# Reordering the opening of a fused attention and two-layer MoE kernel: q, k and v before most weights

## The chip, the core and the metric

The kernel runs on one core of a Trainium2 chip. The time is the device time of one execution in microseconds, and the median of three runs is what counts. Engines: PE is the matrix engine, DVE the vector engine, ACT the scalar engine, POOL the GpSimd engine; SP issues most of the transfers, ACT's queue the rest.

## What is computed

Three stages follow one another on 4608 tokens of width 512:

```python
# attention inside chunks of 64 tokens, 8 batches x 8 heads x 576 tokens x 64
scores = matmul(q_c, k_c^T) / sqrt(64);  scores -= max(scores)
attn = exp(scores);  attn /= sum(attn) + 1e-9
x = matmul(attn, v_c)                      # 4608 x 512 after the heads are put side by side
# gated layer, 512 -> 1536 -> 512
xn = x / sqrt(mean(x*x) + 1e-6) * rms_g
y = (silu(xn @ w_gate) * (xn @ w_val)) @ w_out
# second layer, 512 -> 2048 -> 512
h = y @ w_in;  out = (h * clip(h + 3, 0, 6) / 6) @ w_out2
```

The weights come as 64-bit floats. A load brings the raw words, and the kernel turns them into a float32 and splits that in a high and a low part.

## The kernel before

Tokens are worked in nine blocks of 512. Block 0 is the stretch that matters here. Its attention is done first, in four tiles of 128 tokens (class `Att`, `first[0]` to `first[3]`). Then its gated layer runs in a loop over twelve slices f of the hidden width (lines 1208 to 1223), while the attention of later blocks and the conversion of the remaining weights go on beside it. All engines work their instructions in the order of the program, which is written out by hand (`manual_schedule`).

**The opening** follows two lists. `LOADS` is the order of the first transfers on SP's queue: `w` is the next of 36 weight pieces of 512 KB (gate, val and out of slice 0, of slice 1, and so on: piece 3f is gate f, 3f+1 is val f, 3f+2 is out f), `q0` loads q and k of tile 0 (256 KB each), `v0` its v in four transfers. `START` is the order of the steps. A step ending in a digit belongs to that tile: `trans_qk` turns q and k on PE, `out_q` and `out_k` copy them back on ACT, `scores` (PE), `top` and `less` (DVE: maximum, subtraction), `expo` (ACT), `total` (DVE), `share` (POOL), `trans_p` (PE), `out_p` (ACT), `values` (PE), `out_x` and `square` (ACT), `squares` (POOL), `mean` (PE), `root` (ACT), `inv` (DVE), `spread` (PE), `norm` (DVE), `hi` (ACT, writes XH) and `lo` (POOL, writes XL). XH and XL of all four tiles are what block 0's matmuls read.

**Weight conversion** has four stages for a piece: `m` (ACT, `mag`, L164), `b` (DVE, `bits`, four instructions, L171 to L179), `h` (ACT, `hi`, L186) and `l` (DVE, `lo`, L195). A token `Wb1` does the stage for piece 1; `wb1` does it for pieces 2 and 3, which is group 1; group g is pieces 2g and 2g+1, and there are 18 groups. What `START` leaves is done inside block 0 by `prep_a.step()`. The loop has 36 thirds, hk 0 to 35; third 0 of a slice is the gate product, third 1 the val product and then `sg` (silu times val, DVE, L1215) and its split (`ah` on ACT, L975; `al` on POOL, L976), third 2 the down product of the slice before. After each third `tick()` puts out the planned steps of attention and normalisation, and after every even third `step()` puts out, in this order, lo of one group, hi of the next, bits of the next and mag of the next. At the first step the kernel before has groups 0 to 6 begun and groups 0 to 4 finished, so step s (at hk 2s) does lo of group 4+s and bits of group 6+s.

**What else sits in that loop.** The attention of tokens 512 and on goes in pairs of tiles (class `Pair`): pair 2 starts at hk 7, pair 3 at hk 19, pair 4 at hk 31, with `turn_q` and `turn_k` (DVE, L683) first, `scores`, `top`, `less`, `expo` three thirds later, `total` and `share` two later, `trans_p` and `out_p` at +8, `values`, `out_x` and `square` at +9, `squares` at +11. Between the two lists and the loop, the kernel queues on SP 16 further weight pieces, and after each of the first twelve of them four of the 48 small transfers of pair 2's q and k. The normalisation of block 1 (`Rms(1)`) is planned for hk 31 and 32: `halve`, `mean`, two reciprocals and four products on DVE. `sg` has one buffer, so silu of slice f+1 (ACT) waits until `al` of slice f has read it.

```python
for third in range(3):
    if third == 1:
        mm_up(VB, whole(W["val", f]), xs)
        nc.vector.tensor_tensor(s, s, PS[:, VB, :], op=ALU.mult)
        a = split_act(s)
    elif third == 2 and prev is not None:
        mm_down_a(W["out", f - 1], prev, f == 1, False)
    tick()
    if b == 0:
        prep_hook(hk)
```

Of the kernel before, what the change touches and what calls it, by code (L numbers as in the profile page):

```python
# [18 lines left out]
def _f32_of(word):  # L19
# [7 lines left out]


LOADS = """
    w q0 q1 w w w q2 w q3 v0 w v1 w w w v2 w w w v3 w w w w  # L30
""".split()
START = """
    Wm0 Wb0 Wh0 Wl0 Wm1 trans_qk1 trans_qk0 out_q0 out_k0 wm1 Wb1 scores0 top0 Wh1 out_k1 less0 wb1 out_q1 Wl1 expo0
    trans_qk2
    out_q2 total0 scores1 top1 share0 less1 out_k2 scores2 top2 trans_p0 wh1 wl1 trans_qk3 expo1 wm2 less2
    out_p0 values0 total1 expo2 share1 out_q3 trans_p1 total2 out_k3 out_p1 scores3 square0 share2 wb2 top3
    values1 trans_p2 wm3 out_x0 less3 out_x1 square1 squares0 mean0 out_p2 squares1 values2 expo3 mean1 root0
    total3 out_x2 share3 wb3 inv0 wm4 trans_p3 square2 root1 inv1 wh2 out_p3 wb4 values3 out_x3 squares2
    square3 mean2 spread1 norm1 spread0 root2 squares3 mean3 wl2 inv2 root3 wh3 hi1 spread2 norm0 inv3 wm5
    norm2 hi2 lo1 spread3 hi0 lo2 norm3 hi3 lo3 wh4 wm6 lo0 wl3 wb5 wb6 wh5 wl4  # L40
""".split()

STEPS_P = (
# [1619 lines left out]
```

## Time and profile before

| what | value |
|---|---|
| median of three runs | 1726.3 us (1726.11 to 1726.57) |
| the profiled execution | 1722.63 us, of which the span of instructions is 1720.8 us |
| PE busy | 1656.4 us, 96% of the span |
| DVE busy | 1092.9 us, 64% |
| ACT busy | 843.4 us, 49% |
| POOL busy | 493.5 us, 29% |
| mean granted clock of PE | 0.989 of full speed |

The busy shares are means over the whole span. In the page's 40 slices of 43 us each, PE reads 4, 7, 8 and then 9 in every slice but the last, and DVE reads 7, 9, 9, 7 in the first four: the opening looks unlike the rest and has to be read by itself.

### The profile page before, as it was taken

To read this page: it belongs to the slowest core of one execution; us is meant where nothing else is said; L and a number is where in the kernel's file an instruction comes from. 1 tells how busy PE (TensorE), PEld (TensorE's weight loads), DVE (VectorE), ACT (ScalarE), POOL (GpSimd) and SP (SyncE) were. 2 spreads that over 40 slices of the span, in tenths; PEclk is the share of its full clock that TensorE was granted. 3 is DMA by queue.
4 is the path that set the end of the run, shared out by engine and by line. 5 is a ranking of instruction groups with operands and counts; after the bars stand their busy time and mean duration, and the time that the engine had idled before them with its cause. 6 is when DMAs were issued, how large, how long until landed. Compare 5 with 4: busy or idle time off the path is not lost.

```text
span 1720.8 us, 26448 instructions
## 1 busy us (share of the span) xinstructions
PE 1656.4 (96%) x9896; PEld 1355.6 (79%) x9896; DVE 1092.9 (64%) x1548; ACT 843.4 (49%) x1359; POOL 493.5 (29%) x360
## 2 busy tenths in 40 slices
PE   4789999999999999999999999999999999999998
PEld 4568777787887888887887878888888888888887
DVE  7997655757657586666544468548735754773474
ACT  5554434544554544553534324456545554664553
POOL 2322333430224532265224632231014002301310
PEclk8799999999999999999999999999999999999999
DMA  9832676645798768974778867667766676676664
GB/s 251 231 83 53 198 223 181 175 151 181 235 303 256 216 222 282 296 263 161 276 282 297 291 239 242 220 196 228 237 198 219 220 228 187 222 234 204 196 198 145
DMA packets 291839, 375.06 MB, mean 218 GB/s; under 512 B 132864, under 2 KB 215808, under 8 KB 291584
## 3 DMA queue, kind: packets, MB, share of 16 engines
q1 hardware_dynamic: 230272, 303.11, 57.0%
q10 hardware_dynamic: 61440, 70.27, 12.1%
q8 instruction: 78, 1.28, 0.3%
q14 instruction: 49, 0.40, 0.1%
HBM read 292.55 MB, written 80.74 MB: 217 GB/s over the span
## 4 chain that ended last, share of the span: by engine, by line
PE 51%; DVE 1%; DMA 0%; issue 0%; ACT 0%; ACTq 0%; POOL 0%; SPq 0%; DVEq 0%; POOLq 0%
PE PS L932 24%; PE PS L1461 18%; PE PS L921 2%; PE PS L949 1%; PE PS L946 1%; PE PS L947 1%; PE PS L1478 1%; PE PS L954 1%; PE PS L955 1%; PE PS L958 1%; DMA x<-yd 0%; DVE xf L882 0%; DVE xt L1134 0%; DVE sraw L252 0%; DVE sc L243 0%
## 5 line engine op out<-in xcount | busy, mean ns | idle before, releaser
L932 PE MATMUL PS<-xu,wo 128*128 128x512 f32 x1512 | 351.9, 392 | 2.8 <-DVE gu L1239 2.3
L932 PEld LDWEIGHTS PS<-xu,wo 128*128 128x128 f32 x1512 | 281.5, 188 | 64.3 <-DVE gu L1239 3.1
L1461 PE MATMUL PS<-gs,wq 128*128 128x512 f32 x1344 | 308.5, 390 | 0.0
L932 PE MATMUL PS<-xo,wq 128*128 128x512 f32 x1344 | 306.1, 389 | 0.0
L932 PEld LDWEIGHTS PS<-xo,wq 128*128 128x128 f32 x1344 | 252.0, 188 | 52.2
L1461 PEld LDWEIGHTS PS<-gs,wq 128*128 128x128 f32 x1344 | 251.4, 188 | 51.6
L921 PE MATMUL PS<-XH,w 128*128 128x512 f32 x576 | 149.1, 400 | 11.3 <-DVE sg L1215 5.4
L976 POOL TENSOR_TENSOR al<-sg,ah 128x512 fp32r<-128x512 f32 x52 | 80.5, 1548 | 230.4 <-ACT ah L975 226.1
L921 PEld LDWEIGHTS PS<-XH,w 128*128 128x128 f32 x576 | 108.5, 191 | 39.6 <-DVE sg L1215 6.8
L946 PE MATMUL PS<-gs,wd 128*128 128x512 f32 x288 | 113.6, 394 | 2.1 <-DVE gu L1239 1.6
L947 PE MATMUL PS<-gs,wd 128*128 128x512 f32 x288 | 112.2, 389 | 0.0
L1513 POOL TENSOR_TENSOR gt<-gx 128x512 f32<-128x512 f32 x8 | 10.3, 1291 | 306.3 <-DVE gx L1510 306.3
L1235 POOL TENSOR_TENSOR gs<-gu,gs 128x512 fp32r<-128x512 f32 x60 | 84.8, 1432 | 45.9 <-ACT gs L1234 39.6
L1455 DVE TENSOR_TENSOR gs<-gu,gs 128x512 fp32r<-128x512 f32 x88 | 68.2, 794 | 42.0 <-ACT gs L1454 41.2
L1239 DVE TENSOR_TENSOR gu<-gu,PS 128x512 f32<-128x512 f32 x60 | 40.9, 685 | 76.0 <-ACT gu L1321 40.6
L975 ACT CAST ah<-sg 128x512 fp32r<-128x512 f32 x52 | 32.3, 621 | 99.5 <-DVE sg L1215 67.2
L1392 DVE SCALAR_TENSOR_TENSOR gu<-gu,PS 128x512 f32<-128x512 f32 x48 | 32.8, 684 | 72.9 <-ACT gu L1389 72.9
L921 PE MATMUL PS<-XL,w 128*128 128x512 f32 x288 | 78.9, 396 | 0.0
L949 PE MATMUL PS<-gs,wd 128*128 128x512 f32 x288 | 77.1, 390 | 0.8 <-POOL gs L1235 0.8
L1454 ACT CAST gs<-gt 128x512 fp32r<-128x512 f32 x96 | 58.2, 624 | 38.0 <-DVE gt L1582 28.2
L1454 ACT CAST gs<-gu 128x512 fp32r<-128x512 f32 x96 | 57.7, 622 | 24.8 <-DVE gs L1455 17.8
L1513 POOL TENSOR_TENSOR gt<-gu 128x512 f32<-128x512 f32 x24 | 32.5, 1356 | 129.0 <-DVE gu L1510 124.8
(228 smaller groups left out, 2884.9 us busy)
## 6 DMA issues: line engine op xcount, KB each, us to landing
wq<-stash_in SPq DMA_DIRECT2D x128, 512.0 KB
wo<-ops SPq DMA_DIRECT2D x126, 512.0 KB
wq<-sums_out SPq DMA_DIRECT2D x64, 512.0 KB
wq<-stash_out SPq DMA_DIRECT2D x48, 512.0 KB
wd<-keep_out SPq DMA_DIRECT2D x36, 512.0 KB
ops<-w ACTq DMA_DIRECT2D x36, 256.0 KB
yd<-yst SPq DMA_DIRECT2D x18, 512.0 KB
sraw<-in_moe_w_in_dram ACTq DMA_DIRECT2D x16, 512.0 KB
```

Of the source, the lines that this page charges most:

```text
L921: nc.tensor.matmul(ps, w(wi, c), xs[c][xi], start=(i == 0), stop=(i == n - 1))
L932: nc.tensor.matmul(PS[:, bank, :], op[:, wi, c * 128:(c + 1) * 128], x[xi][:, c, :], start=first and i == 0, stop=last and i == 5, skip_gr ...
L946: nc.tensor.matmul(ps, wm[0], a[0], start=first, stop=False)
L947: nc.tensor.matmul(ps, wm[1], a[0], start=False, stop=False)
L949: nc.tensor.matmul(PS[:, banks[m], :], w[:, 0, m * 128:(m + 1) * 128], a[1], start=False, stop=last)
L976: nc.gpsimd.tensor_tensor(lo, t, hi.bitcast(F32), op=ALU.subtract)
L1235: nc.gpsimd.tensor_tensor(w[:, 1, :], t, w[:, 0, :].bitcast(F32), op=ALU.subtract)
L1239: nc.vector.tensor_tensor(o, x, y, op=op)
L1454: nc.scalar.copy(w[:, 0, :], x)
L1455: e.tensor_tensor(w[:, 1, :], x, w[:, 0, :].bitcast(F32), op=ALU.subtract)
L1461: nc.tensor.matmul(PS[:, banks[m], :], op[:, wi, m * 128:(m + 1) * 128], x[xi], start=first and (wi, xi) == (0, 0), stop=False, skip_group ...
L1513: nc.gpsimd.tensor_tensor(slot(i, "t"), slot(i, "12"), slot(i, "11"), op=ALU.subtract)
```

## The change

Only the two lists change; no instruction is added or dropped. In `LOADS` the q and k of all four tiles and all of v come after at most three weight pieces, and the other thirteen pieces follow. In `START` the steps of attention stand as early as their inputs allow and nearly all conversion tokens stand behind them. Pieces 0 and 1 are converted as before; of the pairs, mag goes to group 3 instead of 6, bits to 2 instead of 6, hi to 1 instead of 5, and lo of groups 1 to 4 is no longer there. So step s of the loop now does lo of group 1+s, hi of 2+s, bits of 3+s and mag of 4+s, three groups (six pieces) behind the kernel before, and ends with lo of group 17 at hk 32 instead of hk 26.

```diff
 LOADS = """
-    w q0 q1 w w w q2 w q3 v0 w v1 w w w v2 w w w v3 w w w w
+    w q0 q1 q2 w q3 v0 w v2 v1 v3 w w w w w w w w w w w w w
 """.split()
 START = """
-    Wm0 Wb0 Wh0 Wl0 Wm1 trans_qk1 trans_qk0 out_q0 out_k0 wm1 Wb1 scores0 top0 Wh1 out_k1 less0 wb1 out_q1 Wl1 expo0
-    trans_qk2
-    out_q2 total0 scores1 top1 share0 less1 out_k2 scores2 top2 trans_p0 wh1 wl1 trans_qk3 expo1 wm2 less2
-    out_p0 values0 total1 expo2 share1 out_q3 trans_p1 total2 out_k3 out_p1 scores3 square0 share2 wb2 top3
-    values1 trans_p2 wm3 out_x0 less3 out_x1 square1 squares0 mean0 out_p2 squares1 values2 expo3 mean1 root0
-    total3 out_x2 share3 wb3 inv0 wm4 trans_p3 square2 root1 inv1 wh2 out_p3 wb4 values3 out_x3 squares2
-    square3 mean2 spread1 norm1 spread0 root2 squares3 mean3 wl2 inv2 root3 wh3 hi1 spread2 norm0 inv3 wm5
-    norm2 hi2 lo1 spread3 hi0 lo2 norm3 hi3 lo3 wh4 wm6 lo0 wl3 wb5 wb6 wh5 wl4
+    Wm0 trans_qk0 out_q0 out_k0 scores0 Wb0 trans_qk1 out_q1 out_k1 top0 less0 Wh0 scores1 expo0 trans_qk2
+    out_q2 out_k2 top1 less1 expo1 total0 share0 scores2 trans_p0 top2 less2 expo2 out_p0 trans_qk3 total1
+    total2 share1 values0 out_q3 Wl0 out_k3 scores3 out_x0 top3 square0 less3 trans_p1 out_p1 Wm1 squares0 expo3
+    values1 share2 square1 out_x1 trans_p2 out_p2 squares1 mean0 total3 share3 Wb1 values2 root0 out_x2 square2
+    trans_p3 out_p3 squares2 mean1 root1 inv0 values3 square3 spread0 inv1 out_x3 norm0 squares3 mean2 root2
+    spread1 inv2 norm1 hi0 lo0 mean3 root3 spread2 inv3 norm2 hi1 lo1 spread3 hi2 Wh1 norm3 Wl1 lo2 hi3 lo3 wm1
+    wb1 wm2 wh1 wm3 wb2
 """.split()
```

## Rows read from the trace of the kernel before

**Rows 1.** Busy time by stretch (length, then each engine; granted clock, transfer share, GB/s).
```profile
0.00:56.30 56.30, 25.34 (x320) 20.89 (x320) 43.33 (x91) 29.85 (x55) 13.66 (x24) 0.78 0.96 249
61.90:120.00 58.10, 46.74 (x257) 36.11 (x255) 54.43 (x98) 30.89 (x49) 17.08 (x6) 0.97 0.57 146
120.00:183.50 63.50, 62.88 (x506) 51.17 (x506) 50.61 (x72) 31.87 (x45) 11.78 (x8) 0.97 0.26 56
```

**Rows 2.** Busy time, 24.2 to 56.3: all instructions; on wtmp (DVE, ACT); on w.
```profile
24.20:56.30 32.10, 15.97 (x199) 13.15 (x196) 29.90 (x66) 19.70 (x39) 11.47 (x13) 0.61 0.97 266
24.20:56.30 32.10, 15.49 (x24) 5.07 (x8) 0.61 0.97 266
24.20:56.30 32.10, 0.00 (x0) 0.00 (x0) 3.40 (x5) 2.57 (x5) 0.00 (x0) 0.61 0.97 266
```

**Rows 3.** PE in order of time: start, length, line, operation [idle before, releaser].
```profile
24.26 1.85 PE L507 MATMUL PS<-ident,q 128*128 128x128 f32 x8
56.31 3.78 PE L921 MATMUL PS<-XH,w 128*128 128x512 f32 x8 [1.92 <-ACT XH L623]
119.95 1.99 PE L763 MATMUL PS<-qT,v 64*64 64x64 f32 x64 [3.00 <-ACT qT L751]
157.62 1.16 PE L763 MATMUL PS<-qT,v 64*64 64x64 f32 x64
166.11 1.07 PE L921 MATMUL PS<-XL,w 128*128 128x512 f32 x4
173.70 1.98 PE L921 MATMUL PS<-XH,w 128*128 128x512 f32 x8
```

**Rows 4.** DVE in order of time, the same columns.
```profile
68.52 0.68 DVE L1215 TENSOR_TENSOR sg<-sg,PS 128x512 f32<-128x512 f32 x1
89.33 1.20 DVE L683 STREAM_TRANSPOSE kT<-k 128x1024 f32<-128x1024 f32 x1
111.61 0.67 DVE L1215 TENSOR_TENSOR sg<-sg,PS 128x512 f32<-128x512 f32 x1
119.03 0.69 DVE L1215 TENSOR_TENSOR sg<-sg,PS 128x512 f32<-128x512 f32 x1 [1.78 <-ACT sg L1211]
143.40 1.28 DVE L195 TENSOR_TENSOR w<-wraw,w 128x512 fp32r<-128x512 f32 x2
144.60 0.76 DVE L171 TENSOR_SCALAR wtmp<-wtmp 128x512 f32<-128x512 f32 x2
148.35 1.21 DVE L731 TENSOR_REDUCE sm<-p 128x16 f32<-128x1024 f32 x1
152.83 0.67 DVE L1215 TENSOR_TENSOR sg<-sg,PS 128x512 f32<-128x512 f32 x1
157.80 0.69 DVE L1215 TENSOR_TENSOR sg<-sg,PS 128x512 f32<-128x512 f32 x1 [3.09 <-PE PS L921]
167.28 0.69 DVE L1215 TENSOR_TENSOR sg<-sg,PS 128x512 f32<-128x512 f32 x1 [4.29 <-PE PS L921]
176.11 2.74 DVE L882 SCALAR_TENSOR_TENSOR xf<-xf,g_sb,rt 128x512 f32<-128x512 f32 x4
```

**Rows 5.** POOL in order of time: `al` of slices 4 and 5.
```profile
113.02 5.34 POOL L976 TENSOR_TENSOR al<-sg,ah 128x512 fp32r<-128x512 f32 x1 [5.63 <-ACT ah L975]
120.49 1.56 POOL L976 TENSOR_TENSOR al<-sg,ah 128x512 fp32r<-128x512 f32 x1 [2.13 <-ACT ah L975]
```

**Rows 6.** ACT in order of time: the copy behind silu of slice 5.
```profile
118.89 1.01 ACT L751 COPY qT<-PS 128x1024 f32<-128x1024 f32 x1
```

**Rows 7.** Transfers in order of time: issues on SP, and a PE load that waited.
```profile
5.57 1.05 SPq L491 DMA_DIRECT2D q<-in_k_dram  x1
10.44 2.42 PEld L507 LDWEIGHTS PS<-ident,q 128*128 128x128 f32 x12 [0.24 <-DMA q<-in_k_dram]
50.22 0.39 SPq L157 DMA_DIRECT2D wraw<-in_moe_w_gate_dram  x1
76.81 2.80 SPq L668 DMA_DIRECT2D k<-in_k_dram  x4
```

## Prediction

> **What bounds the kernel now.** I read the busy time by stretch first, because the 96% of PE is a mean over stages [rows 1]. From 120 to 183.5 us PE works 62.88 of 63.50 us; before 120 it is idle for 31.0 of the first 56.3 us and 11.4 of the 58.1 from 61.9 to 120. So nearly all that can be won in block 0 lies before 120 us. DVE is the other engine to look at: it works 43.33 of the first 56.3 us and 54.43 of the 58.1 after 61.9. The second view is each engine in order of time. PE starts block 0's first product at 56.31, when XH is there [rows 3]. The product of slice 0 on DVE (`sg`) comes at 68.52, and later ones at 111.61, 119.03 and 152.83 with DVE busy without a gap in most of the stretches between [rows 4]. PE's last long wait in block 0 ends at 119.95 [rows 3]. So from 24 us to about 153 us DVE sets the pace, and only from `sg` of slice 9 (157.80, where DVE waits 3.09 us for PE) is PE ahead in the argument, with DVE idle in places. Where the work is paced by DVE, a conversion that is moved is not saved: it must fit into a later hole of DVE, and be done before PE asks for its piece.
>
> I use "old time" below for a moment of the trace of before; the new moment is the old one, less the shift of the head, plus what the tail adds.
>
> **Part 1, the head: the start of block 0.** Between 24.2 and 56.3 DVE is busy 29.90 us, of which 15.49 are `bits` and 3.40 are `lo` that lie wholly inside, 18.9 together [rows 2]. The new list keeps `bits` of one piece and `lo` of two in that place, about 15.49/6 + 2*0.68 = 3.9 us. So DVE work falls by 15.0 us; and tile 3's turn, at 24.26 now [rows 3], can stand some 4 us earlier, since only the loads and three tiles' first steps precede it. Floor for the first product: 56.31 - 15.0 - 4 = 37. But then DVE no longer bounds the opening, and a chain through PE, ACT, POOL and DVE does, with a wait at each step; nothing in the trace shows that chain bare. The upper end is that only half of the 19 us is won: 46.8. I take 43, two thirds of the gain, 13.3 us. The loads allow it: the last of q and k of tile 1 was issued by 6.62 and PE had it at 10.44 [rows 7], and the pace of 249 GB/s [rows 1] brings the 4.7 MB up to v of tile 3 by some 22 us.
>
> Behind the last `norm`, DVE now has `bits` of groups 1, 2 and 3 and `lo` of group 1 ahead of `sg` 0. One burst of `bits` is 148.35 - 144.60 = 3.75 us and one `lo` pair 144.60 - 143.40 = 1.2 us [rows 4], so 3*3.75 + 1.2 = 12.45, with XH's start about 1 us before. Now it is 68.52 - 56.31 = 12.2 from first product to `sg` 0; new about 13.5. Head at `sg` 0: 13.3 - 1.3 = 12.0 us (8 to 17).
>
> **Part 2, what catches the head: k of pair 2.** The steps of slices 0 to 7 do the same amount of conversion as before, three groups behind, so DVE's intervals there stay. But after `sg` 2 DVE turns q and k of pair 2, and these transfers have not moved. They stand on SP behind all of `LOADS`, 48 of them between twelve weight pieces; the last four are issued from 76.81 to 79.61 [rows 7]. From the piece at 50.22 to the one just ahead of 76.81 these are nine rounds of one piece and four small transfers, 2.9 us a round, of which the issues alone are 0.39 and 2.80 in the rows shown: SP's own pace, not that of a waiting engine. The bytes before it are the same, so I leave it where it is. Landing is between at once and 3.8 us after the issue (6.62 to 10.44, [rows 7]); I take 81. DVE asks for k at 89.33 now [rows 4] and would at 77.3 after the change. It waits 3.7 us, and everything queued behind it on DVE waits too: `lo` and `bits` of the next step, `sg` 3, and by them PE's val product of slice 3. Of the head 89.33 - 81 = 8.3 us is left (5.9 with a landing at 83.4; 11.7 at 77.6). This is the term that I trust least.
>
> **Part 3, the tail: where the six pieces are paid.** At hk 22 the old kernel does its last `bits`; the new one has `bits` of groups 15, 16 and 17 at hk 24, 26, 28 and `lo` up to hk 32.
> - hk 24: 3.75 us before `sg` 8, old time 152.83 becomes 156.6.
> - hk 26: `sg` 8 is now followed by `lo` and `bits`, as `sg` 4 is now. There `al` on POOL takes 5.34 us [rows 5], against 1.56 in the slice after; silu of the next slice waits for it, and `sg` 5 comes 119.03 - 111.61 = 7.42 us after `sg` 4 [rows 4]. Old `sg` 9 comes 4.97 after `sg` 8. So `sg` 9 moves to 164.0. Behind silu on ACT stands the copy `out_p` (118.89 in that place, [rows 6]), behind it PE's `values` of the pair: 0.92 us after `sg` 5 starts [rows 3]. Here `values` of pair 3 would go from 157.62 to 164.9, 7.3 us. PE, stalled, may also fall from 2.4 to 1.2 GHz, as it did around 119.95: a mean of 0.97 over 63.5 us [rows 1] is 3.8 us at the lower level and 1.9 us lost, of which I charge 1.5. PE: +8.8 us.
> - hk 28: `bits` of group 17 after `sg` 9 and before the `squares` of pair 3, under PE work: nothing more.
> - hk 32: `lo` of group 17, which holds val of slice 11, stands on DVE behind block 1's whole normalisation. Old: `sg` 10 starts at 167.28, the last `norm` ends at 178.85 [rows 4], 11.6 us. PE's val of slice 10 ends at 167.2 and val of slice 11 starts at 173.70 [rows 3], 6.5 us. New: val of slice 11 needs 11.6 + 0.6 = 12.2 us. PE waits 5.7 us, or 4.8 if its first four matmuls, which read only the high part, may go ahead. The old lateness of `sg` 11 cost PE nothing, so nothing comes back. A clock dip after such a wait: 0 to 1.5.
> Tail: 8.8 + 4.8 to 5.7 + 0 to 1.5, that is 13.6 to 16.0; I take 14.3.
>
> On the page "SBUF — State Buffer" of the Trainium skill, section "SBUF: two separate sides", a DVE and a POOL instruction that want the shared ports exclude each other for one whole instruction. Read so, `al` would lose one DVE instruction and not a burst of eight; the 5.34 us row speaks against it, the 1.56 us row for it. By the rule the tail would be about 4 us shorter, which is one part of the second rival below.
>
> **Part 4, after block 0.** The rest moves as a whole with its start. Later pairs' transfers come earlier against block 1, which may take away some waits; the gain lies between 0 and 2 us. I take 1.
>
> **The sum.** -8.3 + 14.3 - 1 = +5.0 us. The profiled execution is 1722.63 us, a span of 1720.8 and 1.8 around it, 3.7 us below the median; the sum is put on the median: 1726.3 + 5 = 1731.3, forecast 1731.
>
> **Rival 1, about even.** k of pair 2 is there in time, because SP comes through the reordered loads sooner: head 12 to 13, tail 13.6 to 14.3, 0 to 1 back: 1725 to 1728. For it: SP's pace is not bound by compute. Against it: SP issues much the same number of transfers.
>
> **Rival 2, faster.** DVE holds PE less at the end: `al` of slice 8 escapes the burst as the 1.56 us row does [rows 5]. Then only the 3.75 us before `sg` 8 count, and 4.8 at slice 11: tail 8.5. With a head of 12 and 1 back: 1726.3 - 12 + 8.5 - 1 = 1721.8. It is decided where the head exceeds the tail; the price of `al` is 5.34 - 1.56 = 3.8 us, that of `values` and the clock the rest. For it: half of such rows are short. Against it: the long row has the very sequence of steps that the new slice 8 gets.
>
> **Rival 3, the opening does not come forward.** q, k and v in a row land late or the chain is no faster: first product at 46.8 or later, head 5.9 or less, tail 16: 1736 and more.
>
> **How the numbers follow.** Forecast (1728.5 to 1735) 0.48, rival 3 0.06, rival 1 0.26, rival 2 0.20. A measurement of this kernel can tell about 0.2%, 3.5 us, from no change. Slower by more: most of the forecast and rival 3, 0.52; within: rival 1 and the edge of the forecast, 0.29; faster: rival 2 less its edge, 0.19. The range goes from 1720 to 1737, taking in rival 2's time and the landing and clock bounds.
>
> **What would show it.** Right: first product near 43; a wait of DVE of 2 to 5 us for k of pair 2 near 77 to 81; `al` of slice 8 over 5 us and PE waiting for `values` of pair 3; PE idle some 5 us before val of slice 11, released by `lo`; block 1 starting 4 to 7 us after the old 183.5. Wrong: no wait for k, or `al` of slice 8 near 1.6 us, or the first product before 38, and then the time would be nearer the rivals.

## The result

The changed kernel takes 1736.95 us against 1726.33 us (medians of five executions each). The ratio on record is 1.0054 (9.3 us), with a 95% interval of 1.0034 to 1.0074: slower by 5.9 to 12.8 us. It is not the quotient of the medians, which lie 10.6 us apart; here and below, a distance between two times in us is that of their medians. The forecast was 1731 with a range up to 1737: the sign and the mechanisms were right, and the size was about half. That 1736.95 falls 0.05 us inside the range is luck: two of the five executions lie above it (1731.76 to 1739.59). The profiled execution of the changed kernel is its median, with a span of 1735.1 us. The names are those of before; every line number behind `START` is one lower (`sg` is L1214, `lo` L194, `turn_k` L682).

Busy time by stretch of the changed kernel, in the columns of [rows 1]: up to the first product, the second stretch of [rows 1], and from 120 us to the start of block 1.

```profile
0.00:38.96 38.96, 22.45 (x320) 18.44 (x320) 23.11 (x54) 21.16 (x39) 14.05 (x25) 0.96 0.86 222
61.90:120.00 58.10, 39.46 (x272) 30.96 (x272) 45.82 (x81) 25.58 (x41) 13.27 (x6) 0.83 0.61 159
120.00:195.60 75.60, 64.38 (x437) 51.26 (x436) 63.05 (x96) 37.06 (x55) 14.94 (x8) 0.90 0.28 55
```

The opening is shorter by 17 us. From 61.9 to 120 PE works 39.46 us where it worked 46.74, and from 120 us on, where it had been busy 62.88 of 63.50, it is idle for 11.2. Its granted clock in the two stretches is 0.83 and 0.90, against 0.97 in both before [rows 1].

PE of the changed kernel in order of time (start, length, line, operation; in brackets the idle time before it and what ended it), beside [rows 3]:

```profile
38.96 3.78 PE L920 MATMUL PS<-XH,w 128*128 128x512 f32 x8 [1.95 <-ACT XH L622]
73.08 1.16 PE L920 MATMUL PS<-XH,w 128*128 128x512 f32 x4 [0.84 <-DVE sg L1214]
85.97 2.07 PE L920 MATMUL PS<-XH,w 128*128 128x512 f32 x4 [11.73 <-DVE w L194]
115.23 1.99 PE L762 MATMUL PS<-qT,v 64*64 64x64 f32 x64 [4.52 <-ACT qT L750]
160.80 1.98 PE L762 MATMUL PS<-qT,v 64*64 64x64 f32 x64 [4.51 <-ACT qT L750]
...
178.98 1.07 PE L920 MATMUL PS<-XH,w 128*128 128x512 f32 x4
184.80 2.08 PE L920 MATMUL PS<-XH,w 128*128 128x512 f32 x4 [4.75 <-DVE w L194]
...
195.61 1.98 PE L920 MATMUL PS<-XH,w 128*128 128x512 f32 x8
...
201.10 1.98 PE L920 MATMUL PS<-XH,w 128*128 128x512 f32 x8
```

These are the first product of block 0 (before: 56.31), val of slice 3 in two pieces (its first four matmuls at 73.08, the rest at 85.97), `values` of pairs 2 and 3 (before: 119.95 and 157.62), val of slice 11 in two pieces (before: 173.70 in one), and the first and the third product of block 1. In the kernel before these two are:

```profile
183.56 3.01 PE L921 MATMUL PS<-XH,w 128*128 128x512 f32 x8 [0.21 <-ACT XH L910]
...
190.23 1.98 PE L921 MATMUL PS<-XH,w 128*128 128x512 f32 x8
```

DVE of the changed kernel in order of time, beside [rows 4]:

```profile
53.21 0.67 DVE L1214 TENSOR_TENSOR sg<-sg,PS 128x512 f32<-128x512 f32 x1
72.86 1.23 DVE L682 STREAM_TRANSPOSE qT<-q 128x1024 f32<-128x1024 f32 x1
84.10 1.25 DVE L682 STREAM_TRANSPOSE kT<-k 128x1024 f32<-128x1024 f32 x1 [10.01 <-DMA wraw<-in_moe_w_val_dram]
106.89 0.68 DVE L1214 TENSOR_TENSOR sg<-sg,PS 128x512 f32<-128x512 f32 x1
114.31 0.69 DVE L1214 TENSOR_TENSOR sg<-sg,PS 128x512 f32<-128x512 f32 x1 [1.78 <-ACT sg L1210]
152.46 0.68 DVE L1214 TENSOR_TENSOR sg<-sg,PS 128x512 f32<-128x512 f32 x1
159.88 0.69 DVE L1214 TENSOR_TENSOR sg<-sg,PS 128x512 f32<-128x512 f32 x1 [1.78 <-ACT sg L1210]
181.40 2.74 DVE L881 SCALAR_TENSOR_TENSOR xf<-xf,g_sb,rt 128x512 f32<-128x512 f32 x4
184.06 1.29 DVE L194 TENSOR_TENSOR w<-wraw,w 128x512 fp32r<-128x512 f32 x2
```

`sg` 0 is 15.3 us sooner than before. Then q of pair 2 is turned at 72.86, and DVE stands for 10.01 us ahead of `turn_k` at 84.10. Of the 15.3 us, 5.2 are left there (89.33 before) and 4.7 at `sg` 4 and 5. At `sg` 8 it is 0.4, at `sg` 9 the changed kernel is 2.1 us behind. The profile puts the long wait down to a weight piece; which transfer it was, the first experiment shows.

POOL and SP of the changed kernel, beside [rows 5] and [rows 7]: `al` of slices 0, 4, 5, 8 and 9, and the last issue of k of pair 2.

```profile
54.62 5.34 POOL L975 TENSOR_TENSOR al<-sg,ah 128x512 fp32r<-128x512 f32 x1 [13.73 <-ACT ah L974]
...
108.30 5.35 POOL L975 TENSOR_TENSOR al<-sg,ah 128x512 fp32r<-128x512 f32 x1 [5.63 <-ACT ah L974]
115.78 1.56 POOL L975 TENSOR_TENSOR al<-sg,ah 128x512 fp32r<-128x512 f32 x1 [2.13 <-ACT ah L974]
153.87 5.35 POOL L975 TENSOR_TENSOR al<-sg,ah 128x512 fp32r<-128x512 f32 x1 [5.63 <-ACT ah L974]
161.34 1.56 POOL L975 TENSOR_TENSOR al<-sg,ah 128x512 fp32r<-128x512 f32 x1 [2.13 <-ACT ah L974]
...
78.37 2.27 SPq L667 DMA_DIRECT2D k<-in_k_dram  x4
```

What PE waited for between 38 and 205 us of the changed kernel (line, releaser: us in total, times, longest):

```profile
PE PS L920 <- DVE w L194: 16.5, 2, 11.7
PE PS L762 <- ACT qT L750: 9.0, 2, 4.5
```

The first line is two waits for `lo`: val of slice 3 (11.7) and val of slice 11 (4.75). The second is `values` of pairs 2 and 3, 4.5 us each; before it was one wait of 3.00 us [rows 3]. So three stalls and their clock, with 4.4 us of `bits` that now stand ahead of `sg` 8, undo a head of 15 us and add some 11.

**Behind block 0.** The first and the last store of y (the gated layer's result, which the second layer reads back) in the trace of the changed kernel, and then of the kernel before with only pair 2's queue altered (the sixth experiment, which moves nothing in block 0, and whose profile at 1726.07 us lies at the median of the kernel before):

```profile
314.51 3.93 SPq L983 DMA_DIRECT2D yd<-yst  x2
...
1017.70 0.92 SPq L983 DMA_DIRECT2D yd<-yst  x2
```

```profile
305.08 3.97 SPq L984 DMA_DIRECT2D yd<-yst  x2
...
1007.06 0.92 SPq L984 DMA_DIRECT2D yd<-yst  x2
```

The distance is 9.4 us at the first store and 10.6 at the last; the medians differ by 10.6. Nearly all that the change costs is made by the first store, in block 0 and block 1. The profiled execution of before is 3.7 us quicker than its median, and that part comes after its first store (305.27).

### The profile page after: what moved, and what is told of

It is laid out like the page before. It is cut to its first block, busy times and chain, and to the rows that moved or that the text cites. A ratio compares the mean times of both kernels' runs of the same rounds, so it can differ in the third digit from the quotient of the medians.

```text
span 1735.1 us, 26438 instructions
## 1 busy us (share of the span) xinstructions
PE 1662.1 (96%) x9896; PEld 1359.1 (78%) x9896; DVE 1093.1 (63%) x1548; ACT 843.8 (49%) x1359; POOL 495.4 (29%) x360
## 4 chain that ended last, share of the span: by engine, by line
PE 50%; DVE 1%; DMA 0%; issue 0%; ACT 0%; ACTq 0%; POOL 0%; SPq 0%; DVEq 0%; POOLq 0%
PE PS L931 24%; PE PS L1460 18%; PE PS L920 2%; PE PS L948 1%; PE PS L945 1%; PE PS L946 1%; PE PS L1477 1%; PE PS L953 1%; PE PS L954 1%; PE PS L957 1%; DMA x<-yd 0%; DVE xf L881 0%; DVE xt L1371 0%; DVE xt L1133 0%; DVE sraw L251 0%
## 5 line engine op out<-in xcount | busy, mean ns | idle before, releaser
L975 POOL TENSOR_TENSOR al<-sg,ah 128x512 fp32r<-128x512 f32 x52 | 84.2, 1620 | 257.9 <-ACT ah L974 238.5
L920 PEld LDWEIGHTS PS<-XH,w 128*128 128x128 f32 x576 | 108.9, 192 | 55.9 <-DVE w L194 19.1
```

The costliest lines, as they stand in the source:

```text
L920: nc.tensor.matmul(ps, w(wi, c), xs[c][xi], start=(i == 0), stop=(i == n - 1))
L975: nc.gpsimd.tensor_tensor(lo, t, hi.bitcast(F32), op=ALU.subtract)
```

## The experiments

The theory after the result: three terms make the time, namely k of pair 2, which is too late for the earlier start; `al` on POOL of slice 8, kept out by a burst of DVE; and `lo` of group 17, which stands behind block 1's normalisation. The rival: the loss lies in the lists themselves, in the loads or in six conversions that cost more inside the loop than ahead of it. Each experiment is an edit of the changed kernel, but for the sixth. The kernel before ran beside each; its medians were 1724.81 us (first to fourth) and 1726.36 us (fifth to eighth). So a time is read as its distance to the kernel before beside it. The ratios differ by up to 0.0014 from the quotients of the medians.

| experiment | median us | before beside it | ratio, 95% interval | block 1, third product |
|---|---|---|---|---|
| the change itself | 1736.95 | 1726.33 | 1.0054 (1.0034 to 1.0074) | 201.10 |
| 1 k queued earlier | 1729.29 | 1724.81 | 1.0025 (1.0014 to 1.0037) | 192.07 |
| 2 `lo` first at hk 32 | 1732.58 | 1724.81 | 1.0045 (1.0027 to 1.0062) | 196.24 |
| 3 conversions back in front | 1727.38 | 1724.81 | 1.0012 (1.0001 to 1.0024) | 190.39 |
| 4 old order of loads | 1735.62 | 1724.81 | 1.0059 (1.0043 to 1.0075) | 201.19 |
| 5 `al` of slices 4 and 8 on DVE | 1731.21 | 1726.36 | 1.0024 (1.0012 to 1.0036) | 196.86 |
| 6 before, k queued earlier | 1725.87 | 1726.36 | 1.0002 (0.9989 to 1.0015) | 189.75 |
| 7 = 1 and 2 | 1725.19 | 1726.36 | 0.9989 (0.9980 to 0.9999) | 187.83 |
| 8 = 1, 2 and 5 | 1720.63 | 1726.36 | 0.9953 (0.9936 to 0.9970) | 182.31 |

**1. k of pair 2 queued earlier.** Eight small transfers behind each weight piece instead of four, so that q and k need six rounds and not twelve.

```diff
             prep_a.fill(36, 1)
-            some(4)
+            some(8)
```

> The changed kernel, with one edit: eight instead of four small transfers of pair 2's q and k are queued behind each of the further weight pieces, so all 48 are issued after six pieces. Theory (DVE's 10.0 us wait for k of pair 2 sets what of the head is left): k is there when DVE asks for it near 74 us, sg of slice 3 comes near 80 instead of 90.2, the tail stays, the span falls by 9 to 11 us: 1725 to 1728. Rival (the tail is set by something else, a moment in absolute time, and the wait is hidden): the wait goes and block 1 still starts near 195, 1735 to 1738. If the landing of k is also what makes the times of the changed kernel scatter over 8 us, the scatter here is under 2 us.

DVE and SP of this kernel: `turn_k` of pair 2, and the last issue of k.

```profile
75.31 1.25 DVE L682 STREAM_TRANSPOSE kT<-k 128x1024 f32<-128x1024 f32 x1 [1.11 <-DMA k<-in_k_dram]
...
69.62 3.97 SPq L667 DMA_DIRECT2D k<-in_k_dram  x8
```

The wait falls from 10.01 us to 1.11 and `turn_k` comes 8.8 us sooner, released now by k itself. So the long wait was for k, which is all that `turn_k` reads, and not for the weight piece that the profile named. `sg` 3 comes at 81.40, `sg` 4 gains 9.3 us (97.63), block 1 gains 9.0, and the distance to before falls from 10.6 to 4.5 us: by block 1, the largest single cause. The time, 1729.29 us, lies above the 1725 to 1728 that were expected, and the gain of 6.1 us under the 9 to 11: both stalls of the tail stay (at `values` and at slice 11, at most 4.6 and 4.7 us). Another part was wrong too: the executions don't agree better without the wait. They spread over 6.8 us (1725.35 to 1732.16), and those of the kernel before over 9.3.

**2. `lo` of group 17 ahead of the normalisation.** At hk 32 the step of the conversion goes out before `tick()`.

```diff
+                    if b == 0 and hk == 32:
+                        prep_hook(hk)
                     tick()
-                    if b == 0:
+                    if b == 0 and hk != 32:
```

> The changed kernel, with one edit: at hk 32 the conversion step goes ahead of the planned steps, so lo of group 17 stands ahead of block 1's normalisation on DVE. Theory (val of slice 11 waits 4.75 us for that lo and then runs at the lower clock): the wait goes, block 1 starts 5 to 7 us sooner, 1730 to 1732. Rival (another wait takes its place, sg of slice 11 or XH of block 1 behind the later normalisation): at most 2 us sooner, 1735 to 1737.

PE of this kernel, val of slice 11 (without a wait) and the first product of block 1:

```profile
178.51 1.98 PE L920 MATMUL PS<-XH,w 128*128 128x512 f32 x8
...
189.59 2.99 PE L920 MATMUL PS<-XH,w 128*128 128x512 f32 x8 [0.37 <-ACT XH L909]
```

Val of slice 11 is one group of eight again and the wait of 4.75 us is gone. Block 1's third product comes 4.9 us sooner, its first 6.0 (189.59 against 195.61; the normalisation now ends 0.37 us late); 0.5 us of either was there at val of slice 11 already (178.51 against 178.98), ahead of the edit. The distance to before falls from 10.6 to 7.8 us. The intervals of the two ratios overlap, and 1732.58 us lies above the 1730 to 1732 expected, so that the gain is shown in block 0 and not by the time.

**3. The six conversions put back in front.** The tokens that the change dropped are appended to `START`, behind the new order of attention.

```diff
-    wb1 wm2 wh1 wm3 wb2
+    wb1 wm2 wh1 wm3 wb2 wl1 wh2 wm4 wb3 wl2 wh3 wm5 wb4 wl3 wh4 wm6 wb5 wl4 wh5 wb6
```

> The changed kernel's transfers and order of attention, with the conversions that it moved put back ahead of the loop, at the end of the opening (bits up to group 6, lo up to group 4). Theory (a conversion moved is not saved; DVE sets the pace): first product still near 39, but sg of slice 0 at 53.2 + 15 = 68, DVE's wait for k gone, no wait at slices 8 and 11; block 1 starts within 2 us of 183.5 and the time is that of before, 1724 to 1728. Rival (the early start of PE is worth something in itself): under 1722.

What PE waited for in this kernel (38 to 205 us), and `sg` 0 on DVE:

```profile
PE PS L920 <- ACT sg L1210: 19.4, 2, 19.1
...
67.50 0.67 DVE L1214 TENSOR_TENSOR sg<-sg,PS 128x512 f32<-128x512 f32 x1
```

The first product still comes at 38.38, but PE then stands for 19.1 us in one piece, and `sg` 0 is back at 67.50 (before 68.52). All three stalls of the change are gone (what is left at `values` is one wait of 3.1 us, as before), and block 1 starts as before (183.72 against 183.56). So an early first product by itself is worth about 1 us at `sg` 0 and nothing at the start of block 1: DVE's work before 153 us is the same wherever it stands. The time is 2.6 us over before (interval 0.2 to 4.1), which block 0 doesn't explain. By itself this run fits the rival too (conversions that cost more inside the loop); the eighth, with the conversions left in the loop, does not.

**4. The new steps with the old order of loads.**

```diff
-    w q0 q1 q2 w q3 v0 w v2 v1 v3 w w w w w w w w w w w w w
+    w q0 q1 w w w q2 w q3 v0 w v1 w w w v2 w w w v3 w w w w
```

> The changed kernel with the old order of transfers; the order of steps is the new one. Theory (k of pair 2 absorbs what the opening gains or loses): v of tile 3 lands near 38, first product near 45 and sg of slice 0 near 60 instead of 53.2, but DVE's wait for k shrinks by the same, sg of slice 3 stays near 89 to 91, time 1734 to 1739. Rival (every us of the opening counts): 1741 to 1745.

```profile
50.11 3.41 PE L920 MATMUL PS<-XH,w 128*128 128x512 f32 x8 [1.95 <-ACT XH L622]
...
64.35 0.68 DVE L1214 TENSOR_TENSOR sg<-sg,PS 128x512 f32<-128x512 f32 x1
85.16 1.20 DVE L682 STREAM_TRANSPOSE kT<-k 128x1024 f32<-128x1024 f32 x1
```

On PE and DVE of this kernel the first product comes 11.2 us and `sg` 0 11.1 us later than in the changed kernel (4 to 5 us later than expected), yet `turn_k` only 1.1 us, and without a wait; block 1's third product differs by 0.1 us and the time by 0.5 permille, inside the intervals. Without an earlier k, the new order of loads buys nothing past 84 us.

**5. `al` of slices 4 and 8 on DVE.** `split_act` takes the engine as an argument.

```diff
-                        a = split_act(s)
+                        a = split_act(s, nc.vector if b == 0 and f in (4, 8) else nc.gpsimd)
```

> The changed kernel, with one edit: in slices 4 and 8 of block 0 the subtraction al is done by DVE instead of POOL. Theory (al on POOL, kept out for 5.35 us by the burst of conversions on DVE, holds silu, then out_p, then values of the pair: PE waits 4.5 us near 115 and near 160): both waits shrink to under 1 us; the first is given back because sg of slices 6 to 8 is paced by DVE; the second is worth 3 us at the start of block 1; time 1732 to 1735 beside a kernel before of 1725 to 1726. Rival (DVE pays for it: some 1.3 us more in each slice, and it sets the pace anyway): no gain, 1735 to 1738.

What PE waited for at `values`, and POOL's `al` of slice 9, in this kernel:

```profile
PE PS L762 <- ACT qT L750: 2.0, 2, 1.8
...
158.76 5.31 POOL L975 TENSOR_TENSOR al<-sg,ah 128x512 fp32r<-128x512 f32 x1 [12.62 <-ACT ah L974]
```

The two waits of 4.5 us shrink to 2.0 us in all (one is still 1.8, where under 1 was expected), `sg` 9 comes at 157.28 instead of 159.88, and block 1's third product 4.2 us sooner (3 expected). The time lies just under the expected 1732 to 1735. The distance to before falls from 10.6 to 4.9 us, 1.5 us more than block 0 explains, which is within the intervals. `al` on POOL is long again, one slice on (5.31 us, slice 9), but there nothing waits for it in time.

**6. The kernel before with k queued earlier**, the edit of the first experiment.

> The kernel before with pair 2's q and k queued eight behind each further weight piece instead of four. Theory (there k landed at 82 and DVE asks for it at 89.3, so nothing waits): within 2 us of the kernel before. Rival (the earlier small transfers are worth something in themselves, or delay weight pieces): 3 us or more to either side.

It measures 1725.87 against 1726.36 us, no difference, and `turn_k` on DVE stands at 88.99, without a wait:

```profile
88.99 1.20 DVE L683 STREAM_TRANSPOSE kT<-k 128x1024 f32<-128x1024 f32 x1
```

k was in time before the change. Its lateness is made by the earlier start and is no loss that the kernel had.

**7. The first and the second together.**

> The changed kernel with both edits of the first two runs: k of pair 2 early, and the conversion step ahead of the planned steps at hk 32. Theory (the two losses lie one after the other and add): the third product of block 1, at 192.1 with k early alone, 196.2 with the step ahead alone and 190.2 in the kernel before, starts near 187; time 1 to 4 us under the kernel before. Rival (with one loss gone, the other's wait is covered): near 191 or later, no faster than before.

Block 1's third product comes at 187.83, 13.3 us sooner than in the changed kernel; the two alone gave 9.0 and 4.9. The time, 1725.19 us, is 1.2 us under before, as expected but barely clear of it (interval 0.2 to 3.5).

**8. All three together.**

> The changed kernel with all three edits: k of pair 2 early, the step ahead at hk 32, al of slices 4 and 8 on DVE. Theory (the head of 14 us stays, of the tail of 16 us about 9 go): third product of block 1 at 183 to 186 instead of 190.2, time 4 to 7 us under the kernel before. Rival (what is won in block 0 is lost in later blocks): block 1 starts so much sooner, but the time is within 2 us of the kernel before.

PE of this kernel, `values` of pair 3 and block 1's first and third product; SP, the first and the last store:

```profile
148.49 1.16 PE L762 MATMUL PS<-qT,v 64*64 64x64 f32 x64 [1.78 <-ACT qT L750]
...
175.65 2.99 PE L920 MATMUL PS<-XH,w 128*128 128x512 f32 x8 [0.39 <-ACT XH L909]
...
182.31 1.98 PE L920 MATMUL PS<-XH,w 128*128 128x512 f32 x8
...
297.91 3.95 SPq L983 DMA_DIRECT2D yd<-yst  x2
...
1002.68 0.92 SPq L983 DMA_DIRECT2D yd<-yst  x2
```

This version beats both: 1720.63 us, 5.7 us under before by the medians (4 to 7 expected); the ratio of 0.9953 (0.9936 to 0.9970) makes it 5.2 to 11.0 us. Block 1's third product is 7.9 us sooner than in the trace of before, a little more than expected. Against the stores of the sixth experiment it leads by 7.2 us at the first and 4.4 at the last, so in these two traces some 3 us of what block 0 wins is lost in the later blocks; which wait takes it was not tried. Nor was the fifth experiment's edit tried on the kernel before, where `al` of slice 4 takes 5.34 us too [rows 5] and `values` waits 3.00 us. So how much of the 5.7 us is owed to the new order, and how much to that edit alone, is open.

## Why the prediction was right in kind and short in size

Forecast +5.0 us, measured +10.6. By the terms of the sum:

- **The head was undersized.** The first product came at 38.96, near the floor of 37 and not at 43, two thirds of the way; `sg` 0 won 15.3 us and not 12.0. DVE is busy only 23.11 of the first 38.96 us, so it no longer bounds the opening, and the chain through the engines is quicker than I allowed. v of tile 3 was not in by 22 us, for its last issue on SP ended at 26.10; no wait for v in the opening was longer than 0.2 us. The interval from the first product to `sg` 0 was 14.25 us (13.5 predicted). By the mark I had set, a first product before 38, this just missed pointing to a rival. It changed nothing, since part 2 absorbed it.
- **k of pair 2 was the right catch and the worst-sized term**, as the text said it might be. "I take 81" failed: `turn_k` ran at 84.10. Two steps were off in one direction. "The bytes before it are the same, so I leave it where it is": SP's last issue of k moved from 76.81 to 78.37, and its end from 79.61 to 80.64, 1.0 us later. And the landing, for which I took 1.4 us after that end between bounds of 0 and 3.8, was 3.5 (80.64 to 84.10, where `turn_k` starts). The landing 3.1 us later cost the sum 3.1; the asking 3.2 us sooner (74.1, not 77.3) only lengthened the wait, 10.0 us where 3.7 stood. Left of the head were 5.2 us at `turn_k` and 4.7 at `sg` 4, below the 5.9 that I gave as the low end. (The other end, 11.7, would need k to land at 77.6, ahead of the end of its issue at 79.61; at once makes 9.7.) The first experiment shows that the mechanism is this one.
- **The tail was right step by step.** With the head of 4.7 us taken off: `sg` 8 +4.4 (3.75 predicted); `al` of slice 8 5.35 us, as the 5.34 of slice 4 said [rows 5], and `sg` 9 +6.8 (6.2); `values` of pair 3 +7.9 (7.3); `lo` of group 17 a stall of 4.75 us, the low end, because the first four matmuls did go ahead. The start of block 1 is at +16.8 where 14.3 was taken and 16.0 was the upper end. Of the 2.5 us more, 0.6 was there at `sg` 8. The rest is the clock, charged 1.5 us behind `values` and 0 to 1.5 behind slice 11: from `values` to val of slice 11 the delay grows from 7.9 to 10.0, and from there to block 1's first product it grows by 2.0 on top of the 4.75 us stall.
- **Block 1 gave back 2.9 us, by its first store**, where 1 stood and 2 was the upper end: +12.05 at its first product, +10.9 at its third, +9.2 at 314.51 against 305.27. The first 1.0 us of it is block 1's first product itself, which takes 3.01 us in the kernel before, with XH just in time, and 1.98 in the changed one.

The sum with the measured terms: -4.7 + 16.8 - 2.9 = +9.2 at the first store, as the trace has it. The last 1.4 us up to 10.6 come later and belong to no term; executions of one kernel differ by more than that. Of the signs that I had set, every wait came at the step that was named, but the one for k was 10.0 us and not 2 to 5, and block 1 started 12.05 us late and not 4 to 7.

The rivals. The first (even, k in time) is the first experiment in its condition: with k in time the kernel is 4.5 us slower and not even, since the tail costs more than I had it. The second stood on a short `al` in slice 8; it was long, and the fifth experiment, which makes that wait short, gives back 4.2 us in block 0 (the text had 3.8 for `al` and more for what hangs on it). The third, that the opening would not come forward, fell at once. Its low limit of the head, 5.9 or less, and its time, 1736 and more, were met all the same by another cause.

**The clock**, which is what the tail lacked. Busy time of the changed kernel in three stretches that follow a stall (columns as in [rows 1]; the granted clock is the third from the end), and two matmuls of the same shape, in the second stretch and behind it:

```profile
115.00:123.00 8.00, 7.76 (x81) 6.45 (x82) 8.00 (x12) 4.94 (x8) 1.56 (x1) 0.62 0.28 63
...
160.80:166.00 5.20, 5.20 (x73) 4.41 (x74) 5.20 (x10) 3.54 (x5) 1.56 (x1) 0.54 0.22 35
...
184.80:191.00 6.20, 6.20 (x76) 4.75 (x77) 2.09 (x3) 1.57 (x2) 0.90 (x1) 0.63 0.41 66
```

```profile
163.31 0.63 PE L946 MATMUL PS<-ah,w 128*128 128x512 f32 x1
...
173.00 0.39 PE L946 MATMUL PS<-ah,w 128*128 128x512 f32 x1
```

Behind each stall of 4.5 to 4.75 us PE runs for some 5 us at or near the lower of its two levels, 1.2 GHz instead of 2.4: a matmul of 0.39 us takes 0.63. By the growth of the delay above, each of these two stalls of the tail cost some 2 us on top of its own length.

## What to carry to other kernels

Where one engine paces a stretch, moving its work later only pays if each moved piece is followed to the hole it lands in; here all three stalls lay at places where a step was queued behind something longer: a load behind twelve weight pieces, a subtraction on POOL behind a burst of DVE, a conversion behind a normalisation. An opening that is brought forward must bring the next stage's loads forward with it, or their landing time becomes the new start. Repair all the late steps together before judging such a change: alone each repair left it slower than before, the first two together made it about even, and all three made it 5.7 us faster.

## What the hardware did that was not expected

- **POOL waits out a whole burst in some slices and one instruction in others.** `al` of slice 8 starts at 153.87 and ends at 159.22; DVE's ten instructions `lo` (two) and `bits` (eight), back to back from 153.06, end at 158.09. So `al`, which takes 1.3 us where DVE leaves it alone, ended 1.13 us behind the burst. In slice 9 it ends at 162.90, 1.13 us after the pair of `lo` that ran beside it (161.77), and DVE's next pair takes 1.83 us where the same pair in slice 8 takes 0.75: there DVE waited (the two pairs, slice 8 and slice 9, on DVE of the changed kernel, stand below). The section "SBUF: two separate sides" of the page "SBUF — State Buffer" of the Trainium skill has the two engines exclude each other for one instruction; the exclusion agrees, but the rows of slices 0, 4 and 8 show POOL passed over at every change of instruction until DVE pauses. With `al` of slices 4 and 8 moved to DVE, the long one appears in slices 5 and 9. One thing goes with it in all ten traces, wherever `lo` and `bits` stand behind `sg`: `al` is long (5.30 to 5.38 us) where DVE came to `sg` without a pause, and short (1.55 to 1.64) where DVE had waited 1.78 to 1.82 us ahead of `sg`. Whether that decides who is passed over was not tried.

```profile
154.26 0.75 DVE L170 TENSOR_SCALAR wtmp<-wtmp 128x512 f32<-128x512 f32 x2
...
161.69 1.83 DVE L170 TENSOR_SCALAR wtmp<-wtmp 128x512 f32<-128x512 f32 x2
```

- **A product need not wait for its whole piece.** Four matmuls of val of slice 3 ran at 73.08, 11.7 us ahead of the rest; they read only the high part. The same happened at slice 11 (178.98). By the sum of the prediction, the stall there would else have been 5.7 us and not 4.75.
- **Executions of one kernel spread by up to 13 us**, the kernel before over 1721.2 to 1732.3 us and the fifth experiment over 1727.2 to 1739.8. The slowest of the latter has a granted clock of 0.983 over the span, the quickest 0.991; in the kernel before the two go together less closely (1732.29 and 1726.51 us, both at 0.982). The cause was not tried. Single profiles can therefore be compared inside block 0, to about 2 us (seven traces with the same opening have their first product at 38.3 to 40.3), and not by their ends.
